# Three weight rows loaded in halves and prepared earlier, in an attention kernel with two fused MLP layers

## The chip, the cores and the metric

The kernel runs on 1 core of one Trainium2 chip. The metric is the device time of one execution in microseconds (us), as the median of repeated runs. All numbers are float32, and the matrix products are made up of float32r passes.

## What is computed

```python
# 4 batches x 8 heads x 576 positions x 64
scores = scale * q @ k.T
ret = scores * Dmat            # Dmat[n, m] = gamma_h ** (n - m) for m <= n, else 0
x = (ret @ v)                  # -> 2304 tokens x 512
h = x @ w1_in;  g = max(h, 0) + alpha * min(h, 0);  x = g @ w1_out     # 512 -> 2048 -> 512
h = x @ w2_in;  g = h * sigmoid(1.702 * h);         x = g @ w2_out     # 512 -> 2048 -> 512
```

## The kernel before

**Attention.** The 32 heads are worked in 16 pairs, numbered 0 to 15. A pair `i` has three pieces of TensorE (PE) work: `a_scores` (tile `sc`), `a_outer` (tile `st`, the running state) and `a_values` (tile `av`). The loop is staggered: in turn `i` PE does scores and outer of pair `i` and then values of pair `i-1`. VectorE (DVE) takes the scores out of PSUM (`a_evac`, tile `r`), then makes the sums of states (`a_sums`, three short instructions), then takes out the values of the pair before (`a_out`, tile `xs`). ScalarE (ACT) scales the keys (`a_keys`, tile `kts`), which the larger part of `a_outer` needs, and takes out the states. For the first eight pairs, `xa_split` also makes the two parts `x` of the result, high on ACT and the rest on DVE. The PSUM tile of `av` has one buffer, so the values of a pair can't start before `a_out` of the pair before is done. The data of pair `i+3` are asked for in turn `i` behind the values (`a_load`: `ld` of 864 KB, `kts` of 256 KB), since `ld` has four buffers.

**Weight rows.** The weights come as 64-bit floats. A row `(layer, m)` is 128 x 1024 of them (1 MB): 128 columns of the first product and 128 rows of the second. It is loaded into `raw` (two buffers) and converted with 32-bit operations, in this order: `w_abs` on ACT (called abs below), `w_clamp` on DVE (two instructions, clamps), `w_top` and `w_low` on DVE (top, low), `w_hi` on ACT (hi: the rounded high part) and `w_lo` on DVE (lo: the rest). A matmul group of 12 uses the high part in its first two matmuls and the rest in its third.

**First layer.** The steps behind the attention are numbered from 0. Step `s` does the first product of one row for one chunk of 512 tokens (`mm1`, tile `h`, 12 matmuls), the activation (two ACT instructions and one DVE instruction, tile `g`), a split of `g` into two parts (`gs`), and the second product of step `s-2` (`mm2`, tile `acc`, 12 matmuls). Steps 0 to 2 use rows 0, 1 and 2 for the first chunk. Steps 3 to 10 use rows 0 to 7 for the second, so row 3 is first used in step 6, row 6 in step 9 and row 7 in step 10. Steps 11 to 18 go back to rows 3 to 10 for the first chunk.

**Order.** Each engine works its instructions in the order in which the program gives them. The main loops stand in a fixed order. The conversions hang in a list of events with a time each (`at`), counted in pairs, then in steps from `base = 17`. `run_to(t)` works off all events up to `t`, at three places of a pair and at two of a step. All loads go through the one queue of SyncE (SP), where an instruction that waits holds up those behind it.

Of the kernel before, what the change touches and what calls it, by code (L numbers as in the profile page):

```python
# [14 lines left out]
DM, DFF = 512, 2048  # L15
# [18 lines left out]
def kernel(  # L34
# [12 lines left out]
    nc = tc.nc  # L47
# [38 lines left out]
    def at(time, fn, *args):  # L86
        events.append((time, len(events), fn, args))
# [7 lines left out]
    wt, raws, cvs, x_t = {}, {}, {}, {}  # L95
    both = "p (c n) -> p c n"

    def w_load(key, src):
        raws[key] = cvp.tile([128, 2 * DM, 2], I32, tag="raw", name="raw", bufs=2)
        nc.sync.dma_start(out=raws[key], in_=src[key[1]].rearrange("p (f t) -> p f t", t=2))  # L100

    def w_abs(key):
        cvs[key] = cvp.tile([128, 2 * DM], F32, tag="cv", name="cv", bufs=2)
# [32 lines left out]

    def w_words(t, key, src, ahead, d):
        at(t - ahead, w_load, key, src)
        for i, fn in enumerate((w_abs, w_clamp, w_top, w_low)):
            at(t + d * i, fn, key)  # L140

# [264 lines left out]
    wz = att.tile([128, 128], F32, name="wz")  # L406
    n_a = len(PAIRS)
    base = n_a + 1
    pace = [6.0, 11.0, 15.6]
    pace += [base + t for t in (1.3, 2.9, 4.5, 6.0, 7.2, 8.8, 10.6, 12.4, 14.2, 16.0, 17.8, 19.6, 22.2)]  # L410
    ahead = {0: 2.2, 1: 2.2, 2: 2.2}
    for m, t in enumerate(pace):
        d = 0.75 if m < 2 else 0.5
        w_words(t, (1, m), w1, ahead.get(m, 1.6), d)
        at(t + 3 * d + 0.25, w_hi, (1, m))
        at(t + 4 * d + 0.25, w_lo, (1, m))
# [9 lines left out]
    with tc.manual_schedule():  # L426
# [46 lines left out]
        for n, (layer, c, m0, _) in enumerate(BLOCKS[N_FIRST:], 1):  # L473
            homes[layer, c] = xp[n % 2]
            for k in range(NK):
                t = starts[layer, c, m0] - (4 if n == 1 else 6) + (0.9 if n == 1 else 1.3) * k
# [5 lines left out]
        for m in range(NM):  # L482
            t = (26.2, 29.4, 32.6)[m] if m < 3 else 35.2 + 1.6 * (m - 3) if m < 11 else 48.5 + 3 * (m - 11)
            w_words(base + t, (2, m), w2, 1.6, 0.5)
            at(base + t + 1.8, w2_store, (2, m))
            t = n1 - NM + m + LAG + 1
            at(t - 1, w2_load, (2, m))
            at(t + 0.5, w_hi, (2, m))
            at(t + 0.9, w_lo, (2, m))
# [75 lines left out]
```

## Time and profile before

| | before |
|---|---|
| median of 3 runs | 886.39 us (884.36 to 887.72) |
| the profiled execution | 891.64 us, of which the traced span is 889.6 us |
| PE busy | 871.3 us (98%) |
| DVE busy | 391.2 us (44%) |
| ACT busy | 340.5 us (38%) |
| GpSimd (POOL) busy | 174.4 us (20%) |
| bytes moved | 95.53 MB, 107 GB/s over the span |
| mean granted TensorE clock | 0.99 of full speed |

Times inside the trace are counted from the start of the span. The shares are means over the whole span. The program has stages with different limits, so a stage is read by its own rows.

### The profile page before, as it was taken

To read this page: it belongs to the slowest core of one execution; us is meant where nothing else is said; L and a number is where in the kernel's file an instruction comes from. 1 tells how busy PE (TensorE), PEld (TensorE's weight loads), DVE (VectorE), ACT (ScalarE), POOL (GpSimd) and SP (SyncE) were. 2 spreads that over 40 slices of the span, in tenths; PEclk is the share of its full clock that TensorE was granted. 3 is DMA by queue.
4 is the path that set the end of the run, shared out by engine and by line. 5 is a ranking of instruction groups with operands and counts; after the bars stand their busy time and mean duration, and the time that the engine had idled before them with its cause. 6 is when DMAs were issued, how large, how long until landed. Compare 5 with 4: busy or idle time off the path is not lost.

```text
span 889.6 us, 12276 instructions
## 1 busy us (share of the span) xinstructions
PE 871.3 (98%) x5036; PEld 739.5 (83%) x5036; DVE 391.2 (44%) x501; ACT 340.5 (38%) x602; POOL 174.4 (20%) x141
## 2 busy tenths in 40 slices
PE   8988898999999999999999999999999999999998
PEld 8877687888888888898888888888888888888898
DVE  3877686777455777572344312211221121112211
ACT  4633564554444444354455422222222222222222
POOL 0000000001222233222332322222222222222221
PEclk9989999999999999999999999999999999999999
DMA  7875652334275565642333300020002000100000
GB/s 272 319 258 199 204 186 98 143 142 142 71 249 177 161 192 191 214 167 95 107 129 106 109 1 25 0 71 1 24 0 72 1 25 0 60 1 13 23 26 24
DMA packets 30535, 95.53 MB, mean 107 GB/s; under 512 B 3600, under 2 KB 8848, under 8 KB 26000
## 3 DMA queue, kind: packets, MB, share of 16 engines
q1 hardware_dynamic: 30480, 94.76, 31.2%
q8 instruction: 39, 0.64, 0.3%
q14 instruction: 16, 0.13, 0.1%
HBM read 71.16 MB, written 23.59 MB: 107 GB/s over the span
## 4 chain that ended last, share of the span: by engine, by line
PE 89%; DVE 4%; DMA 2%; issue 2%; ACT 2%; SPq 0%; POOL 0%; ACTq 0%; DVEq 0%; POOLq 0%
PE h L326 43%; PE acc L378 42%; PE av L190 2%; DMA raw<-in_w_dram 2%; PE st L190 1%; PE sc L190 1%; DVE cv L125 1%; DMA ld<-in_qkv_dram 1%; PE wps L433 1%; DVE r L224 1%; ACT w L78 0%; DVE xs L269 0%; DVE w L81 0%; DVE cv L118 0%; POOL gs L81 0%
## 5 line engine op out<-in xcount | busy, mean ns | idle before, releaser
L326 PE MATMUL h<-x,w 128*128 128x512 f32 (+1 forms) x1920 | 423.5, 370 | 5.6 <-DVE w L81 4.1
L378 PE MATMUL acc<-gs,w 128*128 128x512 f32 (+1 forms) x1920 | 421.0, 368 | 2.1 <-ACT gs L78 1.6
L326 PEld LDWEIGHTS h<-x,w 128*128 128x128 f32 x1920 | 338.5, 190 | 67.7 <-DVE w L81 5.4
L378 PEld LDWEIGHTS acc<-gs,w 128*128 128x128 f32 x1920 | 337.0, 189 | 62.3 <-ACT gs L78 1.8
L81 POOL TENSOR_TENSOR gs<-g,gs 128x512 fp32r<-128x512 f32 (+1 forms) x137 | 174.2, 1272 | 706.9 <-ACT gs L78 591.0
L345 DVE TENSOR_TENSOR g<-h,g 128x512 f32<-128x512 f32 (+1 forms) x80 | 51.1, 638 | 299.2 <-ACT g L344 299.2
L78 ACT ACTIVATE gs<-g 128x512 fp32r<-128x512 f32 (+1 forms) x160 | 94.0, 588 | 103.0 <-DVE g L340 53.5
L344 ACT ACTIVATE g<-h 128x512 f32<-128x512 f32 (+1 forms) x80 | 44.4, 554 | 228.7 <-PE h L326 228.7
L340 DVE SCALAR_TENSOR_TENSOR g<-h,nalpha_sb,g 128x512 f32<-128x512 f32 (+1 forms) x80 | 55.6, 695 | 120.3 <-ACT h L339 120.2
L338 ACT ACTIVATE g<-h 128x512 f32<-128x512 f32 (+1 forms) x80 | 44.1, 551 | 117.7 <-PE h L326 114.6
L125 DVE SCALAR_TENSOR_TENSOR cv<-raw,cv 128x1024 int32<-128x1024 int32 x32 | 45.6, 1424 | 0.3
L104 ACT ACTIVATE cv<-raw 128x1024 f32<-128x1024 f32 x32 | 36.1, 1129 | 23.2 <-DMA raw<-in_w_dram 13.2
L81 DVE TENSOR_TENSOR x<-xf,x 128x512 fp32r<-128x512 f32 (+1 forms) x32 | 34.6, 1082 | 22.9 <-ACT x L78 22.8
L339 ACT ACTIVATE h<-h 128x512 f32<-128x512 f32 (+1 forms) x80 | 44.0, 550 | 0.0
L118 DVE SCALAR_TENSOR_TENSOR cv<-raw,cv 128x1024 int32<-128x1024 int32 x32 | 42.8, 1339 | 0.2
L108 DVE TENSOR_SCALAR cv<-cv 128x1024 f32<-128x1024 f32 x32 | 24.2, 755 | 9.6 <-ACT cv L104 9.5
L111 DVE TENSOR_SCALAR cv<-cv 128x1024 int32<-128x1024 int32 x32 | 26.4, 825 | 1.1
L78 ACT ACTIVATE w<-cv 128x1024 fp32r<-128x1024 f32 x16 | 16.9, 1057 | 22.4 <-DVE cv L125 22.4
L224 DVE TENSOR_TENSOR r<-sc,diag_sb 128x1024 f32<-128x1024 f32 x16 | 19.5, 1222 | 12.1 <-PE sc L190 11.8
L190 PE MATMUL av<-r,ld 128*64 128x128 f32 (+1 forms) x320 | 22.0, 275 | 0.0
L81 DVE TENSOR_TENSOR w<-w2f,w 128x1024 fp32r<-128x1024 f32 x16 | 19.6, 1224 | 3.6 <-ACT w L78 2.1
L190 PE MATMUL sc<-ld 64*128 64x128 f32 x256 | 19.8, 295 | 0.2 <-DMA ld<-in_qkv_dram 0.2
(38 smaller groups left out, 286.9 us busy)
## 6 DMA issues: line engine op xcount, KB each, us to landing
raw<-in_w_dram SPq DMA_DIRECT2D x32, 1024.0 KB, 6.0
ld<-in_qkv_dram SPq DMA_DIRECT2D x15, 864.0 KB, 6.3
w<-cv SPq DMA_DIRECT2D x16, 512.0 KB, 6.7
w2f<-w SPq DMA_DIRECT2D x16, 512.0 KB, 3.4
kts<-in_kn_dram SPq DMA_DIRECT2D x16, 256.0 KB, 5.8
xf<-x SPq DMA_DIRECT2D x16, 256.0 KB, 3.4
out_dram<-o SPq DMA_DIRECT2D x16, 256.0 KB, 4.2
part<-pt SPq DMA_DIRECT2D x3, 1024.0 KB, 5.0
```

What stands on the lines that cost most here:

```text
L78: return nc.scalar.activation(out=out, in_=in_, func=ACTF.Copy)
L81: return eng.tensor_tensor(out=out, in0=a, in1=b.bitcast(F32), op=ALU.subtract)
L118: nc.vector.scalar_tensor_tensor(out=g, in0=raws[key][:, :, 1], scalar=-(1 << 30), in1=g, op0=ALU.bitwise_and, op1=ALU.bitwise_or,)
L125: nc.vector.scalar_tensor_tensor(out=g, in0=raws.pop(key)[:, :, 0], scalar=29, in1=g, op0=ALU.logical_shift_right, op1=ALU.bitwise_or,)
L190: nc.tensor.matmul(out=out, lhsT=lhsT, rhs=rhs, start=start, stop=stop, skip_group_check=True)
L326: nc.tensor.matmul(out=t, lhsT=w[:, cw, k * 128:k * 128 + 128], rhs=x[:, cx], start=(i == 0), stop=(i == 3 * NK - 1),)
L338: nc.scalar.activation(out=g, in_=t, func=ACTF.Relu)
L339: nc.scalar.activation(out=t, in_=t, func=ACTF.Relu, scale=-1.0)
L340: nc.vector.scalar_tensor_tensor(out=g, in0=t, scalar=nalpha_sb[:, m:m + 1], in1=g, op0=ALU.mult, op1=ALU.add)
L344: nc.scalar.activation(out=g, in_=t, func=ACTF.Sigmoid, scale=1.702)
L345: nc.vector.tensor_tensor(out=g, in0=t, in1=g, op=ALU.mult)
L378: nc.tensor.matmul(out=acc[0][d], lhsT=w[:, cw, d * 128:d * 128 + 128], rhs=g[:, cx], start=(j == m0 and i == 0), stop=(j == m1 - 1 and i ...
```

## The change

Each row of weights is loaded by two transfers of 512 KB instead of one of 1 MB. For rows 0, 1 and 2 the second transfer is asked for one pair after the first. For all others both stand directly behind one another. The list of times for the first layer's rows is another: rows 0, 1 and 2 move from 6.0, 11.0 and 15.6 pairs to 3.6, 8.6 and 14.1, rows 3 to 7 move by 0.2 to 0.6 steps, and rows 12 to 15 by 0.1 to 0.8. Row 2 gets the wider spacing of its operations that rows 0 and 1 have.

```diff
     def w_load(key, src):
         raws[key] = cvp.tile([128, 2 * DM, 2], I32, tag="raw", name="raw", bufs=2)
-        nc.sync.dma_start(out=raws[key], in_=src[key[1]].rearrange("p (f t) -> p f t", t=2))
+        w_piece(key, src, 0)
+
+    def w_piece(key, src, c):
+        f = src[key[1]].rearrange("p (f t) -> p f t", t=2)
+        nc.sync.dma_start(out=raws[key][:, c * DM:c * DM + DM], in_=f[:, c * DM:c * DM + DM])
...
     def w_words(t, key, src, ahead, d):
         at(t - ahead, w_load, key, src)
+        at(t - ahead + (1.0 if ahead > 2 else 0), w_piece, key, src, 1)
...
-    pace = [6.0, 11.0, 15.6]
-    pace += [base + t for t in (1.3, 2.9, 4.5, 6.0, 7.2, 8.8, 10.6, 12.4, 14.2, 16.0, 17.8, 19.6, 22.2)]
-    ahead = {0: 2.2, 1: 2.2, 2: 2.2}
+    pace = [3.6, 8.6, 14.1]
+    pace += [base + t for t in (0.8, 2.35, 3.9, 5.45, 7.0, 8.8, 10.6, 12.4, 14.2, 15.9, 17.6, 19.3, 21.4)]
+    ahead = {0: 2.6, 1: 3.2, 2: 3.2}
     for m, t in enumerate(pace):
-        d = 0.75 if m < 2 else 0.5
+        d = 0.75 if m < 3 else 0.5
```

PE's order of matmuls is the same in both. Three places show how the others move. The first is SP's queue at the start of the attention, before: `ld_187` belongs to pair 3, and the row of weights stands behind the loads of pair 6.

```order
L167 DMA ld_187<-in_qkv_dram 128x1728
L168 DMA kts_116<-in_kn_dram 128x512
L167 DMA ld_245<-in_qkv_dram 128x1728
L168 DMA kts_116<-in_kn_dram 128x512
L167 DMA ld_305<-in_qkv_dram 128x1728
L168 DMA kts_116<-in_kn_dram 128x512
L167 DMA ld_368<-in_qkv_dram 128x1728
L168 DMA kts_116<-in_kn_dram 128x512
L100 DMA raw_387<-in_w1_dram 128x2048
```

The same queue in the change, again from pair 3's load on.

```order
L172 DMA ld_187<-in_qkv_dram 128x1728
L173 DMA kts_116<-in_kn_dram 128x512
L104 DMA raw_206<-in_w1_dram 128x1024
L172 DMA ld_247<-in_qkv_dram 128x1728
L173 DMA kts_116<-in_kn_dram 128x512
L104 DMA raw_206<-in_w1_dram 128x1024
L172 DMA ld_308<-in_qkv_dram 128x1728
L173 DMA kts_116<-in_kn_dram 128x512
```

The first half of row 0 now stands behind pair 3's loads and the second behind pair 4's.

The second place is DVE around row 0, in the change. It begins with the values of pair 3 (`xs_432`), the clamps of row 0 (`cv_377`) and the scores of pair 5 (`r_453`), and ends with low.

```order
L274 TENSOR_TENSOR xs_432<-av_413,otab_sb_82 128x576
L112 TENSOR_SCALAR cv_377<-cv_377 128x1024
L115 TENSOR_SCALAR cv_377<-cv_377 128x1024
L81 TENSOR_TENSOR x_439<-xs_245,x_439 128x64
L229 TENSOR_TENSOR r_453<-sc_442,diag_sb_80 128x1024
L81 TENSOR_TENSOR x_455<-xs_432,x_455 128x512
...
L122 SCALAR_TENSOR_TENSOR cv_377<-raw_206,cv_377 128x1024
L274 TENSOR_TENSOR xs_432<-av_474,otab_sb_82 128x576
L81 TENSOR_TENSOR x_499<-xs_432,x_499 128x64
L229 TENSOR_TENSOR r_513<-sc_502,diag_sb_80 128x1024
L129 SCALAR_TENSOR_TENSOR cv_377<-raw_206,cv_377 128x1024
```

Before, the clamps of row 0 stood ahead of the scores of pair 7, and low stood two pairs further on. On ACT the copy hi of row 0 (`w_531`) now stands ahead of the keys of pair 7, here in the change:

```order
L181 ACTIVATE r_513<-st_516,vtab_sb_78 128x320
L78 ACTIVATE w_531<-cv_377 128x1024
L78 ACTIVATE x_311<-xs_432 128x448
L181 ACTIVATE kts_116<-kts_116,vtab_sb_78 128x4x64 x2
L181 ACTIVATE r_570<-st_573,vtab_sb_78 128x320
```

Before, it stood at the same place of a turn two pairs later, ahead of the keys of pair 9.

The third place is DVE at the end of the attention, before: the values of pairs 14 and 15 (`xs_925`, `xs_1051`), row 2 (`cv_1028`) and the first activation (`g_1078`).

```order
L269 TENSOR_TENSOR xs_925<-av_1008,otab_sb_82 128x576
L108 TENSOR_SCALAR cv_1028<-cv_1028 128x1024
L111 TENSOR_SCALAR cv_1028<-cv_1028 128x1024
L269 TENSOR_TENSOR xs_1051<-av_1032,otab_sb_82 128x576
L118 SCALAR_TENSOR_TENSOR cv_1028<-raw_927,cv_1028 128x1024
L462 TENSOR_SCALAR nalpha_sb_84<-alpha_sb_83 128x16
L340 SCALAR_TENSOR_TENSOR g_1078<-h_1065,nalpha_sb_84,g_1078 128x512
L125 SCALAR_TENSOR_TENSOR cv_1028<-raw_927,cv_1028 128x1024
L81 TENSOR_TENSOR gs_1085<-g_1078,gs_1085 128x512
L81 TENSOR_TENSOR w_1083<-cv_1028,w_1083 128x1024
```

The same place in the change; row 2 is `cv_963` and its rest `w_1061`.

```order
L229 TENSOR_TENSOR r_996<-sc_985,diag_sb_80 128x1024
L112 TENSOR_SCALAR cv_963<-cv_963 128x1024
L115 TENSOR_SCALAR cv_963<-cv_963 128x1024
...
L274 TENSOR_TENSOR xs_933<-av_1015,otab_sb_82 128x576
L122 SCALAR_TENSOR_TENSOR cv_963<-raw_791,cv_963 128x1024
L274 TENSOR_TENSOR xs_1058<-av_1039,otab_sb_82 128x576
L129 SCALAR_TENSOR_TENSOR cv_963<-raw_791,cv_963 128x1024
L467 TENSOR_SCALAR nalpha_sb_84<-alpha_sb_83 128x16
L345 SCALAR_TENSOR_TENSOR g_1085<-h_1072,nalpha_sb_84,g_1085 128x512
L81 TENSOR_TENSOR w_1061<-cv_963,w_1061 128x1024
```

Row 2's clamps moved to between the scores and the sums of pair 15, top ahead of the last values, low ahead of the first activation, and lo ahead of its split.

## Rows read from the trace of the kernel before

**Rows 1.** Windows: first and third of three stretches; busy PE, PEld, DVE, ACT, POOL, granted clock, DMA share, GB/s.

```profile
13.97:85.48 71.51, 66.49 (x1118) 57.92 (x1117) 57.31 (x99) 34.30 (x78) 0.00 (x0) 0.95 0.74 270
...
148.07:889.60 741.53, 736.38 (x3601) 625.22 (x3599) 285.36 (x341) 269.31 (x466) 174.20 (x137) 1.00 0.25 84
```

**Rows 2.** Chain in order of time: start, us, what; undisturbed pair and matmul groups.

```profile
20.03 2.06 PE av L190 x36
22.09 1.09 PE sc L190 x16
23.18 0.88 PE st L190 x20
...
85.48 2.96 PE h L326 x12
...
101.69 2.72 PE h L326 x12
```

**Rows 3.** Waits of PE: total us, times, longest.

```profile
PE h L326 <- DVE w L81: 4.1, 3, 1.6
PE st L190 <- ACT kts L176: 3.8, 2, 2.6
```

**Rows 4.** Chain at the end of row 0, from low on.

```profile
47.63 1.15 DVE cv L125
...
48.80 1.06 ACT w L78
49.85 0.47 ACT x L78
...
50.77 1.51 PE st L190 x16
52.29 3.81 PE av L190 x36
56.09 1.56 PE sc L190 x16
```

**Rows 5.** Windows of 4 us behind two waits of PE; columns as in rows 1.

```profile
52.00:56.00 4.00, 4.00 (x40) 3.46 (x37) 2.15 (x5) 1.79 (x4) 0.00 (x0) 0.50 0.46 186
72.00:76.00 4.00, 2.71 (x48) 2.14 (x43) 3.46 (x6) 1.85 (x3) 0.00 (x0) 1.00 1.03 364
```

**Rows 6.** Chain: DVE's instructions in a row, each up to the next one's start.

```profile
39.47 0.53 DVE x L81
...
65.42 0.61 DVE cv L108
...
66.06 0.69 DVE cv L111
66.75 1.13 DVE r L224
...
68.73 0.71 DVE xs L269
```

**Rows 7.** Window ahead of the first weights; columns as in rows 1.

```profile
16.00:20.00 4.00, 4.00 (x75) 3.51 (x74) 2.86 (x6) 3.50 (x10) 0.00 (x0) 1.00 0.32 98
```

**Rows 8.** Loads issued in 18:19 us: KB each, us to landing.

```profile
ld<-in_qkv_dram SPq DMA_DIRECT2D x1, 864.0 KB, 4.3
kts<-in_kn_dram SPq DMA_DIRECT2D x1, 256.0 KB, 4.5
```

**Rows 9.** Chain: row 0's load, from issue to landing.

```profile
27.01 9.22 DMA raw<-in_w_dram
```

**Rows 10.** Timeline of SP: the issue of that load.

```profile
27.01 0.42 SPq L100 DMA_DIRECT2D raw<-in_w_dram  x1
```

**Rows 11.** Chain: step 0's `g`, and step 2's remaining ten matmuls.

```profile
89.63 0.75 DVE g L340
...
95.03 3.93 PE h L326 x10
```

**Rows 12.** Timeline of ACT: the keys of pair 4.

```profile
25.48 0.89 ACT L176 ACTIVATE kts<-kts,vtab_sb 128x256 f32<-128x256 f32 x2
```

## The prediction

> **What bounds the kernel now.** I read the windows of three stretches first [rows 1]: the attention from 13.97 to 85.48 us, the first steps up to 148.07, and the rest. In the third PE is busy for 736.4 of 741.5 us at the full clock: it is bound by PE, and as PE's matmuls stay the same there is nothing to win there. The other two stretches hold the losses.
>
> *Attention, 13.97 to 85.48.* In the chain an undisturbed pair is scores 1.09, outer 0.88, values 2.06, so 4.03 us [rows 2]. Fifteen pairs and the last values make 15 x 4.03 + 2.06 = 62.5, which would end at 76.5. The end is at 85.48: 9.0 us are lost.
>
> *First steps, 85.48 to 148.07.* In them lie 11 first and 9 second products of 12 matmuls. One takes 2.72 (the first of all 2.96) [rows 2]: 54.6 of 62.6. So 8.0 us are lost.
>
> Next I read what PE waited for [rows 3]: 3.8 us in two waits of outer for the keys from ACT, and 4.1 us in three waits of the first product for lo. The chain shows how the longest wait of the attention comes about [rows 4]. ACT's hi stands ahead of the keys in ACT's queue and needs low from DVE. Low ended at 48.78, hi took 1.06, the split 0.47, then came the keys, and outer could go on at 50.77. PE stood idle before that for 2.6, the longest of the two waits [rows 3]. Behind this wait the granted clock was 0.50 (1.2 GHz) from 52 to 56 [rows 5]: values took 3.81 instead of 2.06, scores 1.56 instead of 1.09, the outer's last 16 matmuls 1.51 instead of 0.7 (16/20 of 0.88), in sum 3.0 us. The second of these waits (3.8 - 2.6 = 1.2) lies in 72 to 76, where the clock stayed at 1.00.
>
> **The change, part by part.**
>
> *Loads.* The same bytes in two transfers. Between 16 and 20 us the DMA engines are busy for only 0.32 [rows 7], and the first half of row 0 now waits there. The second stands behind pair 4's loads, which go out when pair 0's values are done, at 13.97 + 4.03 = 18.0; issues stand 0.42 apart [rows 10], so 18.0, 18.4 and 18.9. The 864 KB of that pair land at 18.0 + 4.3 = 22.3, the 256 KB behind them at 18.4 + 4.5 = 22.9 [rows 8]: 0.6 for 256 KB, so a half row lands about 1.3 later, at 24.2. ACT reaches abs at 25.48, where it took up pair 4's keys before [rows 12]. The next pair's loads go out a pair later, at 22.0, so they find the queue nearly free. A pair asks for 1120 KB, which by that rate take 2.7 of its 4.03 us; a half row of 1.3 just fits in the gap. Before, the whole MB took 9.22 [rows 9] and stood ahead of three pairs' loads. I put the loads at 0. Upper bound: each of the six halves delays a pair by its full 1.3, 7.8 us; lower bound 0. I take 0, as the rows nearest to it are those of a queue that runs empty.
>
> Here a rule speaks against the change. The Trainium skill, "DMA: Bandwidth & Descriptors", section "Rules for kernel authors", asks for 1 MB or more per transfer, and the section on the anatomy of a DMA gives about 2.0 us as fixed cost of each. If 32 more transfers paid it on the path, that would be an estimated 64 us. The trace does not agree for a transfer that follows another: the 0.6 us above hold no such cost.
>
> *Row 0 (pairs 4 to 7).* DVE's pieces, from [rows 6]: clamps 66.75 - 65.42 = 1.33, `r` 1.13, the sums 68.73 - 66.75 - 1.13 = 0.85, `xs` 0.7; low 1.15 [rows 4], and top and lo on the same 1024 columns also 1.15; on ACT hi 1.06 and the split 0.47 [rows 4], the keys 0.89 [rows 12]; a split of 448 columns is 0.53, so 0.6 for 512 and 0.1 for 64. Two points matter for PE: values of pair i are asked for 1.09 + 0.88 = 1.97 after the scores of i+1 start, and need `xs` of the pair before; the keys are asked for about 1.3 after the scores start (1.09 and some 0.2 for four of the outer's 20 matmuls, an estimate from its 0.88).
> Abs, on 1024 columns like hi, puts pair 4's keys at 25.48 + 1.06 + 0.89 = 27.4, where they are asked for (pair 4's scores start at 26.06 = 13.97 + 3 x 4.03): some **0.1**. Pair 5's scores start at 30.2, pair 6's at 34.2. DVE: `xs` of pair 3 ends at 31.1, clamps 32.4, split 32.5, `r` 33.6, split 34.2, sums 35.1, top 36.2, `xs` 36.9. Values of pair 5 were asked for at 36.2: **0.7 waited**. Pair 7 starts at 39.0. DVE goes on: split 37.0, `r` 38.2, low 39.3. On ACT hi ends at 40.4, the split at 40.8, the keys at 41.7; asked for at 40.3: **1.4 waited**. Then DVE catches up. Pair 8 starts at 44.4 (keys 41.7, 0.7 for the outer's rest, values 2.06), pair 9 at 48.4, pair 10 at 52.5.
>
> *Row 1 (pairs 9 to 12).* The same order without the splits from pair 8 on. `xs` of pair 8 ends at 53.3, clamps 54.6, split 55.1, `r` 56.2, sums 57.1, top 58.2, `xs` 58.9, asked for at 56.5 + 1.97 = 58.5: **0.4**. Pair 12 starts at 61.0. Then `r` 60.0, low 61.2, hi 62.2, keys 63.1, asked for at 62.3: **0.8**.
>
> *Row 2 (pair 15).* Its clamps now stand between `r` and sums. Pair 13 starts at 65.8, and pair 15 at 73.9: `r` ends at 76.2, clamps 77.5, sums 78.4, `xs` of pair 14 79.0. The last values are asked for at 77.9: **1.1**.
>
> Sum of waits 0.1 + 0.7 + 1.4 + 0.4 + 0.8 + 1.1 = 4.5, each below the 2.6 that brought the clock down. The attention ends at 76.5 + 4.5 = 81.0 instead of 85.48: **4.4 gained**. Bounds: no wait left, 9.0; as late as before, 0. I take the sum along the queues, since the order on each engine is known and the durations hardly vary.
>
> *First steps.* Call the end of the attention A. Before, low of row 2 stood behind the first `g`, so hi and lo came late, step 2 got its lo at 95.0, and ten matmuls took 3.93 instead of 2.27 at the lowered clock [rows 11]. Now low ends at A + 0.8 + 1.15 = A + 1.9, hi at A + 3.0, the first `g` at A + 4.9 (1.94 behind its product, as before: 90.38 - 88.44, [rows 2, 11]) and lo at A + 6.05. Step 2 starts at A + 2.96 + 2.72 = A + 5.7 and needs lo for its third matmul, 2 x 0.227 later, at A + 6.1: no wait, just. The other two waits for lo, 2.5 together (4.1 - 1.6, [rows 3]), are rows 6 and 7 in steps 9 and 10. Step k starts at A + 11.1 + 5.44 (k - 3). In DVE's new order row 6 has behind `g` of step 7 (A + 37.5) clamps of row 7, the split of `g` (0.6 for 512 columns) and its lo: A + 40.6, wanted at A + 44.2. Row 7's lo stands behind `g` of step 9, which ends 1.94 behind its product, at A + 48.4: A + 49.6, wanted at A + 49.7, just in time. So the 8.0 come back: **8.0 gained**; bounds 5.5 (those 2.5 stay) and 8.0.
>
> *The rest.* SP issues 29 halves more at 0.42 each; PE, busy throughout the third stretch [rows 1], covers SP's time there. I take 0; without that cover it is at most the 12.2 us of 29 x 0.42.
>
> **Sum.** 4.4 + 8.0 = 12.4. The span becomes 889.6 - 12.4 = 877.2, the profiled execution (2.0 more than its span) 891.6 - 12.4 = 879.2. That execution lay 5.25 above the median of the runs, so for the median 886.4 - 12.4 = 874.0.
>
> **Rivals.**
> 1. *The clock falls in pair 7.* The waits of 0.7 and 1.4 lie 4 us apart and might work like one of 2.6. Price 3.0 [rows 4], so 877.0. For it: the waits come close together; against: a single 1.2 cost nothing [rows 5]. The Trainium skill, "TensorE: Matmul & The Clock Gate", Part 1, says that idleness halves the clock and activity restores it; both rows fit that.
> 2. *The change doesn't do what it says in the attention.* A late half row makes abs wait, ACT is late with the keys as before, and the 9.0 stay: only the 8.0 come back, 878.4. For it: a load took 9.22 here [rows 9]; against: half the bytes behind a short queue.
> 3. *All waits vanish.* DVE has more air than I count: 9.0 + 8.0, so 869.4.
> 4. *The halves hold up the pairs' loads*, 7.8 of the 12.4 given back: 881.8. Against it: the idle share [rows 7].
> 5. *Slower: the doubled transfers of the later rows reach the path.* SP is one queue, and weights, stores and chunk loads stand in it. With 29 more transfers at the 0.42 of an issue each the gain is gone (12.2 of 12.4); from 0.57 each on it is over 0.5% slower, and at 1.0 each 886.4 - 12.4 + 29 = 903. For it: all loads share SP; against: DMA share of 0.25 there [rows 1].
>
> **How the numbers follow.** Forecast 0.52, rivals 0.15, 0.10, 0.12, 0.07 and 0.04. 0.5% is 4.4 us, about what a measurement of this kernel can tell from no change. The forecast and rivals 1 to 3 lie beyond it, 0.89, of which I take off 0.02 for mixtures; rival 4 lies on the edge. So faster 0.87, same 0.08, slower 0.05. The range reaches from rival 3 at 869.5 over rival 2 to 880, leaving out rivals 4 and 5 and half of rival 3.
>
> **What would show it.** Right: abs of row 0 starts at about 25.5 without waiting for its load; PE waits once for `xs` and once for keys in pairs 6 and 7, none over 1.5; granted clock 1.00 from 36 to 80; attention ends near 81; step 2 does not wait for lo, nor do steps 9 and 10; step 11 starts 12 us sooner. Wrong: a wait over 2 us with a granted clock of 0.50 behind it, loads of pairs 5 to 12 that take over 8 us, or new waits of PE behind step 11.

## The result, and the profile after

The changed kernel takes 877.31 us (median of 4 runs, 875.46 to 879.47); the kernel before, beside it on the same chip, 886.19 (884.36 to 887.72). The ratio is 0.9901 with a 95% interval of 0.9872 to 0.9931: 8.9 us faster, between 6.1 and 11.3. The forecast of 874.0 is 3.3 too low; the time lies in the range, on the side that was forecast.

The profiled execution took 877.74 us, with a span of 876.0. The windows of the changed kernel, cut at the same places as [rows 1] (the attention; the first steps up to step 11; the rest), with the same columns:

```profile
13.41:81.92 68.51, 64.31 (x1117) 55.63 (x1117) 58.10 (x100) 34.22 (x78) 0.00 (x0) 1.00 0.80 282
81.92:137.16 55.24, 55.24 (x241) 45.09 (x242) 45.12 (x56) 31.71 (x47) 0.00 (x0) 1.00 0.53 181
137.16:876.00 738.84, 734.73 (x3600) 623.56 (x3599) 285.00 (x341) 268.99 (x465) 173.99 (x137) 1.00 0.25 85
```

And the kernel before, cut behind the attention at exactly these places:

```profile
85.48:148.23 62.75, 57.16 (x241) 45.97 (x242) 46.39 (x57) 31.75 (x47) 0.00 (x0) 0.97 0.46 156
148.23:889.60 741.37, 736.22 (x3600) 625.06 (x3599) 285.20 (x341) 269.23 (x465) 174.20 (x137) 1.00 0.25 84
```

The span is 13.6 us shorter: 0.6 by an earlier start of the scores (13.41 in the chain's times, where the kernel before has 14.04; [rows 1] cut it 0.07 earlier), 2.9 in the attention, 7.5 in the first steps, 2.5 in the rest, where nothing was forecast. PE counts as busy for every moment of the first steps now, and the granted clock is 1.00 (2.4 GHz) in all three.

What PE waited for in the changed kernel (us in total, times, longest), beside [rows 3]:

```profile
PE st L195 <- ACT kts L181: 2.2, 4, 0.9
PE av L195 <- DVE xs L274: 2.1, 3, 1.3
...
PE acc L383 <- ACT gs L78: 0.5, 1, 0.5
PE acc L383 <- POOL gs L81: 0.5, 1, 0.5
```

In this view the first product `h` waits for nothing any more, and the wait for keys of 2.6 is gone; several of 0.2 to 1.3 have taken its place (0.4 of the 2.2 lies in the start-up). Where they lie, the timeline of PE shows (start, length; in brackets the idle time and its releaser). The first row is the scores of pair 5, and an undisturbed pair has its scores 4.03 behind the last:

```profile
29.52 1.16 PE L195 MATMUL sc<-ld 64*128 64x128 f32 x16
...
33.55 1.16 PE L195 MATMUL sc<-ld 64*128 64x128 f32 x16
...
35.07 1.08 PE L195 MATMUL st<-ld,kts 128*64 128x64 f32 x16
36.37 0.99 PE L195 MATMUL av<-ld,r 64*64 64x128 f32 x16 [0.22 <-DVE xs L274]
...
38.43 1.16 PE L195 MATMUL sc<-ld 64*128 64x128 f32 x16
...
40.72 1.08 PE L195 MATMUL st<-ld,kts 128*64 128x64 f32 x16 [0.87 <-ACT kts L181]
...
43.79 1.16 PE L195 MATMUL sc<-ld 64*128 64x128 f32 x16
...
47.81 1.16 PE L195 MATMUL sc<-ld 64*128 64x128 f32 x16
...
49.86 1.07 PE L195 MATMUL st<-ld,kts 128*64 128x64 f32 x16 [0.62 <-ACT kts L181]
...
52.92 1.16 PE L195 MATMUL sc<-ld 64*128 64x128 f32 x16
...
59.50 0.99 PE L195 MATMUL av<-ld,r 64*64 64x128 f32 x16 [0.51 <-DVE xs L274]
...
63.25 1.08 PE L195 MATMUL st<-ld,kts 128*64 128x64 f32 x16 [0.27 <-ACT kts L181]
...
79.79 0.99 PE L195 MATMUL av<-ld,r 64*64 64x128 f32 x16 [1.33 <-DVE xs L274]
```

From one row of scores to the next are 4.88, 5.36, 4.02 and 5.11: a wait for keys costs PE more than the idle time in the bracket, as the 16 outer matmuls behind it take 1.08 instead of 0.69. In pair 6 two waits cover each other: its keys were late too, as ScalarE's timeline shows, and ended the outer product 0.56 late, but the values behind it had to wait for `xs` until 36.37 in any case.

```profile
34.51 0.91 ACT L181 ACTIVATE kts<-kts,vtab_sb 128x256 f32<-128x256 f32 x2 [2.23 <-DMA kts<-in_kn_dram]
```

The wait at 49.86 has its cause in the chain:

```profile
39.40 8.77 DMA raw<-in_w_dram
...
48.25 1.16 ACT cv L108
49.41 0.80 ACT kts L181 x2
```

The second half of row 1 left at 39.40 and landed 8.8 us later; abs stood still for it, and pair 9's keys stood behind abs in ScalarE's queue.

### The profile page after: what moved, and what is told of

It is laid out like the page before. It is cut to its first block, busy times and chain, and to the rows that moved or that the text cites. A ratio compares the mean times of both kernels' runs of the same rounds, so it can differ in the third digit from the quotient of the medians.

```text
span 876.0 us, 12331 instructions
## 1 busy us (share of the span) xinstructions
PE 865.2 (99%) x5036; PEld 734.4 (84%) x5036; DVE 390.5 (45%) x501; ACT 340.2 (39%) x602; POOL 174.2 (20%) x141
## 4 chain that ended last, share of the span: by engine, by line
PE 91%; issue 3%; DVE 2%; DMA 1%; POOL 1%; ACT 1%; SPq 0%; POOLq 0%; ACTq 0%; DVEq 0%
PE h L331 43%; PE acc L383 43%; PE av L195 2%; POOL gs L81 1%; DMA raw<-in_w_dram 1%; PE st L195 1%; PE sc L195 1%; DVE r L229 1%; PE wps L438 0%; DVE xs L274 0%; DMA vtab_sb<-in_vtab_dram 0%; DVE cv L122 0%; DVE cv L115 0%; ACT kts L181 0%; DVE cv L112 0%
## 5 line engine op out<-in xcount | busy, mean ns | idle before, releaser
L108 ACT ACTIVATE cv<-raw 128x1024 f32<-128x1024 f32 x32 | 36.2, 1131 | 30.4 <-DMA w<-cv 11.3
```

## The experiments

All times are medians, with ratios to the kernel before on the same chip. "The end of the attention" is the start of the first `h` in the profile's timeline of PE.

**Split alone.** The changed kernel with the old times: only the loads differ from before.

```diff
-    pace = [3.6, 8.6, 14.1]
-    pace += [base + t for t in (0.8, 2.35, 3.9, 5.45, 7.0, 8.8, ...)]
-    ahead = {0: 2.6, 1: 3.2, 2: 3.2}
+    pace = [6.0, 11.0, 15.6]
+    pace += [base + t for t in (1.3, 2.9, 4.5, 6.0, 7.2, 8.8, ...)]
+    ahead = {0: 2.2, 1: 2.2, 2: 2.2}
...
-        d = 0.75 if m < 3 else 0.5
+        d = 0.75 if m < 2 else 0.5
```

> The kernel before with its own times, but every row loaded in two halves (for rows 0 to 2 a pair apart). My theory (the times at which rows are converted matter, the halves don't): 886, within 1.5 us of the kernel before, and the attention still loses about 9 us with a wait over 2 us for the keys. Rival theory (the halves keep the pairs' loads from being held up): 877 to 880, and the keys of the pair behind row 0 are no longer late.

891.08 us, ratio 1.0056 (1.0038 to 1.0073): slower, which neither expected. On ScalarE's timeline abs of row 0 stands still for its load:

```profile
37.49 1.12 ACT L108 ACTIVATE cv<-raw 128x1024 f32<-128x1024 f32 x1 [6.01 <-DMA raw<-in_w_dram]
```

And PE's waits, with a new one for `r`:

```profile
PE st L195 <- ACT kts L181: 4.8, 3, 2.2
...
PE st L195 <- ACT r L181: 1.9, 1, 1.9
```

The half that goes out a pair later holds up abs; behind abs stands `r`, for which the outer product of the next pair now waits 1.9. The halves alone don't help, and at the old times cost 4.2 us.

**Whole loads at the new times.** The changed kernel with one transfer of 1 MB per row.

```diff
-        w_piece(key, src, 0)
+        nc.sync.dma_start(out=raws[key], in_=src[key[1]].rearrange("p (f t) -> p f t", t=2))
...
-        at(t - ahead + (1.0 if ahead > 2 else 0), w_piece, key, src, 1)
```

> The changed kernel with its times, but every row in one transfer of 1 MB. My theory: 877 to 879, at most 1.5 us slower than the changed kernel, from a load of pair 4 or 5 that lands late. Rival theory: most of the gain is gone, 883 or more, with loads of pairs 5 to 12 over 8 us.

877.64, ratio 0.9894 (0.9874 to 0.9914). As the theory said: the times do it, the halves give nothing measurable. In the profile they even cost something: the attention lasts 67.4 with whole loads (13.57 to 80.99) against 68.5, because row 1's load is in time and pair 10's scores stand 4.03 behind pair 9's instead of 5.11. The last short block of the first layer, of which more below, waits longer there, 1.5 instead of 0.5.

**Rows 0 to 2 moved alone.** The changed kernel with the old times of the later rows.

```diff
-    pace += [base + t for t in (0.8, 2.35, 3.9, 5.45, 7.0, 8.8, ...)]
+    pace += [base + t for t in (1.3, 2.9, 4.5, 6.0, 7.2, 8.8, ...)]
```

> The changed kernel, with the times of rows 3 to 15 put back. My theory: the waits of steps 9 and 10 for lo come back, 2.4 us, so 879.5 to 880; attention and step 2 as in the changed kernel. Rival theory (the times of the later rows carry the gain): 884 or more.

879.78, ratio 0.9923 (0.9906 to 0.994), in the expected interval. Its waits hold the two of the first product for lo, in steps 9 and 10, again:

```profile
PE h L331 <- DVE w L81: 2.4, 2, 1.3
```

**Later rows moved alone.** The other half: old times for rows 0 to 2, in halves.

```diff
-    pace = [3.6, 8.6, 14.1]
+    pace = [6.0, 11.0, 15.6]
...
-    ahead = {0: 2.6, 1: 3.2, 2: 3.2}
+    ahead = {0: 2.2, 1: 2.2, 2: 2.2}
...
-        d = 0.75 if m < 3 else 0.5
+        d = 0.75 if m < 2 else 0.5
```

> The changed kernel, with the times of rows 0 to 2 put back, in halves all the same. My theory: the attention loses about 9 us again and step 2 waits for row 2 again, so only some 2.4 us are gained: 883.5 to 884. Rival theory: 878 to 880.

888.06, ratio 1.0008 (0.9991 to 1.0025): missed by 4 us, because the expectation took the halves as free. Against the split alone, its proper neighbour, the later rows gave 3.0; against the pair of runs above 2.5 (879.78 - 877.31), or 2.0 by their ratios. So of the gain some 2 to 3 belongs to the later rows, the bulk to rows 0 to 2.

**hi behind the keys.** ScalarE's queue holds pair k's hi ahead of the next keys; now behind.

```diff
-        at(t + 3 * d + 0.25, w_hi, (1, m))
+        at(t + 3 * d + (0.95 if m < 2 else 0.25), w_hi, (1, m))
```

> The changed kernel, but the hi copies of rows 0 and 1 stand behind the next pair's key scalings on ScalarE instead of ahead of them; nothing else moves. Theory (the state products' waits of 0.87 and 0.27 us for the keys at 40.7 and 63.3 us are time on the path, and ScalarE stands idle for over 2 us ahead of either hi, so the keys take nothing from it): both waits vanish, the end of the attention comes 0.9 to 1.1 us earlier (about 80.9), and the median is 1.0 us under the changed kernel's 877.3, about 876.3. Rival (VectorE's chain of low word, sums and lo is what holds the pair up, and the wait only moves one step on, to the last values): the attention still ends at 81.7 to 81.9 and the median is 877.0 to 877.5.

876.03, ratio 0.987 (0.9843 to 0.9897). The attention lasts 66.9 us (12.11 to 78.97) instead of 68.5, and ScalarE's timeline shows the keys done before the hi begins, so that the keys of pairs 7 and 12 are no longer late: the scores behind these two stand 4.02 and 4.03 apart instead of 5.36 and 4.76. (Waits of 0.2 for the keys of pair 4 and 0.3 for those of pair 9 remain.) The median alone, 1.3 lower, would not show it, as the two intervals overlap.

```profile
36.17 0.89 ACT L181 ACTIVATE kts<-kts,vtab_sb 128x256 f32<-128x256 f32 x2
38.08 1.06 ACT L78 ACTIVATE w<-cv 128x1024 fp32r<-128x1024 f32 x1 [1.02 <-DVE cv L129]
```

**Halves of rows 0 to 2 together, and row 1's halves a pair earlier.** Two kernels that remove the wait for row 1's second half in two ways:

```diff
-        at(t - ahead + (1.0 if ahead > 2 else 0), w_piece, key, src, 1)
+        at(t - ahead, w_piece, key, src, 1)
```

> The changed kernel, but the two halves of rows 0 to 2 go out together at the first half's place; the halves of all later rows stay as they are. Theory (the pair between the halves is what makes row 1's words late, 1.32 us on ScalarE, and what the halves gave came in the first layer's last short block, where a row of the second layer landed in 6.6 us instead of 8.9): the abs of row 1 waits under 0.3 us, the attention ends at about 81.1 as with whole loads, the wait of the accumulation in the last short block stays at 1.0 us or below, and the median is 876.3 to 876.8. Rival (the halves a pair apart are what spares the pairs' own loads, and both halves together hold up the next loads as the whole loads did at the old times): the scores or keys wait over 1 us more, attention end 83 or later, median 878 to 879.

```diff
-    ahead = {0: 2.6, 1: 3.2, 2: 3.2}
+    ahead = {0: 2.6, 1: 4.2, 2: 3.2}
```

> The changed kernel, but both halves of row 1 go out one pair earlier; the pair between them stays. Theory (the second half's landing at 48.2 us is what row 1's abs, and behind it the keys and state products, wait for): the 1.32 us of ScalarE and the 0.62 us of the state products at 49.9 vanish, the attention ends at about 81.2, median 876.6. Rival (the transfer is late because the pairs' loads stand in the same rings; moved forward it delays a pair's keys by as much): the wait of the state products for the keys stays at 2 us in sum, median 877.0 to 878.

878.48 (ratio 0.9897, 0.9872 to 0.9922) and 875.89 (0.9872, 0.9847 to 0.9898). In both abs of row 1 starts without a wait, here in the first:

```profile
48.95 1.15 ACT L108 ACTIVATE cv<-raw 128x1024 f32<-128x1024 f32 x1
```

In the second the scores of pairs 8 to 11 stand 4.03 apart, so the 1.08 between pairs 9 and 10 is gone, as the theory has it. Within the attention the waits for keys sum to 1.1 in the first and 1.5 in the second, against the changed kernel's 1.8, so the rivals' mechanism, more waiting or as much, isn't there, though in the first the rival's time is. The medians can't decide. In the profiled executions, 2.7 apart, the start makes the difference: the scores start at 15.47 in the first and at 12.01 in the second, while the attention lasts 67.4 and 68.1, the other way round. The second's is the longer because an early start is paid for in part: abs of row 0 then comes before the second half of its load and waits 0.57 for it, and pair 4 loses 0.8. (In the kernel with hi behind the keys, which started at 12.11, the same wait is 0.46.)

**Both, and row 7 half a step earlier.**

```diff
-        at(t - ahead + (1.0 if ahead > 2 else 0), w_piece, key, src, 1)
+        at(t - ahead, w_piece, key, src, 1)
...
-    pace += [base + t for t in (0.8, 2.35, 3.9, 5.45, 7.0, 8.8, ...)]
+    pace += [base + t for t in (0.8, 2.35, 3.9, 5.45, 6.5, 8.8, ...)]
...
-        at(t + 3 * d + 0.25, w_hi, (1, m))
+        at(t + 3 * d + (0.95 if m < 2 else 0.25), w_hi, (1, m))
```

> Both edits, hi behind the keys and the halves of rows 0 to 2 together, and row 7 of the first steps half a step earlier (its lo was 0.3 us late at 131.4). Theory (the three gains are on the path and add up, 1.1, 0.8 and 0.3): attention end about 80.1, no stall of h at 131, median 875.1 to 875.5. Rival (one waiting engine hides the next, so that the gains don't add): 876.2 to 877.0. A time of 877.3 or more would say that the new order costs something that none of the single edits shows.

875.44, ratio 0.9863 (0.9836 to 0.9889). The attention lasts 65.5, and the product at step 10 no longer takes 3.02 but 2.72: the gains add up there. Some of it went at a place that the expectation had left out, the last short block of the first layer. On PE's timeline, the kernel before:

```profile
369.53 0.50 PE L378 MATMUL acc<-gs,w 128*128 128x256 f32 x2 [1.60 <-ACT gs L78]
370.54 2.09 PE L378 MATMUL acc<-gs,w 128*128 128x256 f32 x10 [0.50 <-POOL gs L81]
372.43 2.51 PE L326 MATMUL h<-x,w 128*128 128x256 f32 x12
```

The changed kernel there:

```profile
357.38 0.50 PE L383 MATMUL acc<-gs,w 128*128 128x256 f32 x2 [0.51 <-ACT gs L78]
358.38 1.46 PE L383 MATMUL acc<-gs,w 128*128 128x256 f32 x10 [0.50 <-POOL gs L81]
```

And this version:

```profile
355.65 0.50 PE L383 MATMUL acc<-gs,w 128*128 128x256 f32 x2 [1.24 <-ACT gs L78]
356.65 2.32 PE L383 MATMUL acc<-gs,w 128*128 128x256 f32 x10 [0.50 <-POOL gs L81]
358.77 2.28 PE L331 MATMUL h<-x,w 128*128 128x256 f32 x12
```

PE waits for ScalarE's copy of `gs`, which stands behind an abs of the second layer's row 12, which waits for its load. In the kernel before:

```profile
368.06 1.12 ACT L104 ACTIVATE cv<-raw 128x1024 f32<-128x1024 f32 x1 [5.12 <-DMA raw<-in_w_dram]
369.07 0.41 ACT L78 ACTIVATE gs<-g 128x256 fp32r<-128x256 f32 x1
```

Where the wait is long, matmuls behind it run slower (2.09 and 2.32 for the ten that take 1.46 in the changed kernel, 2.51 and 2.28 for twelve that take 1.60). My theory had put its shrinking from 1.60 to 0.51 down to the halves. That fell: this kernel and the one with hi behind the keys load in halves and wait 1.24 and 1.16.

**Row 12 ahead of the stores.** Its load stands in SP's queue behind four x stores that wait for the accumulation, here in the kernel before:

```profile
357.09 2.03 SPq L403 DMA_DIRECT2D x<-o  x4
359.17 1.18 SPq L100 DMA_DIRECT2D raw<-in_w_dram  x1
```

It goes ahead of them, once in the kernel before and once in the joint version:

```diff
-            w_words(base + t, (2, m), w2, 1.6, 0.5)
+            w_words(base + t, (2, m), w2, 2.8 if m == 12 else 1.6, 0.5)
```

> The kernel before with one edit: the load of the second layer's row 12 goes out ahead of the four x stores of the first layer instead of behind them (its step 48.7 instead of 49.9 after the attention); the attention and the first steps stay. Theory (that load, landing 8.9 us after its issue at 359 us, is what the last short block's accumulation waited for, 1.60 us and 0.50 us, and the clock fell behind it): the wait of the accumulation for ScalarE's gs vanishes, and the median is 1.5 to 2.5 us under the kernel before's, about 884.7. Rival (the transfers of that stretch are slow wherever the load is put, or the wait is for VectorE): the wait stays at 1.2 us or above and the median is that of before, 886 to 887.

> The earlier joint version (hi behind the keys, halves of rows 0 to 2 together, row 7 half a step earlier) with the same edit, the second layer's row 12 ahead of the x stores. Theory (the same wait of 1.2 us in that version's profile): no wait of the accumulation for gs in the last short block, median 873.4 to 874.2 against the joint version's 875.4. Rival (that wait comes and goes with the executions and costs little on average): 875.0 to 875.6.

885.45, ratio 0.9984 (0.9963 to 1.0006), and 872.49, ratio 0.9836 (0.9813 to 0.986). In the profile of the first the load goes out at 350.95, ahead of the stores at 355.40. In both the wait for `gs`, POOL's part with it, is gone, and the rest from step 11 on is the same to 0.2 us, 4.1 and 1.7 below the kernels before and after. The kernel before with this edit, the rest:

```profile
146.54:883.80 737.26, 734.21 (x3600) 623.50 (x3599) 285.22 (x341) 269.59 (x465) 174.17 (x137) 1.00 0.25 85
```

The joint version with it:

```profile
135.28:872.40 737.12, 734.03 (x3600) 623.43 (x3598) 285.25 (x341) 269.37 (x465) 173.98 (x137) 1.00 0.26 85
```

In the kernel before the median moved by 1.9, and its interval still holds no change; in the joint version by 2.9 from one measurement to the next, 2.4 by the ratios. The mechanism is shown by the profiles, the size over many executions only as about 2 to 3.

**Words behind the values.** The joint version with row 12, and rows 0 and 1 with a whole pair between their steps, so that VectorE's words stand behind `xs`.

```diff
-        d = 0.75 if m < 3 else 0.5
+        d = (1.0, 1.0, 0.75)[m] if m < 3 else 0.5
...
-        at(t + 3 * d + (0.95 if m < 2 else 0.25), w_hi, (1, m))
+        at(t + 3 * d + 0.25, w_hi, (1, m))
```

> As the one before, and the steps of rows 0 and 1 a whole pair apart (d 1.0 instead of 0.75), so that VectorE's clamps, top and low words each stand behind the last operation on a pair's values instead of ahead of it. Theory (the waits of the values product for VectorE's output of the pair before, 0.79 us at 37 us and 0.51 us at 58 us, are the top words of rows 0 and 1 that stand ahead of it): both vanish, attention 1.1 to 1.3 us shorter, median 872.2 to 873.0. Rival (VectorE has no room in these pairs, the clamps and words then hold up the next scores' eviction or the sums): waits of 0.5 us or more turn up at other pairs and the median stays within 0.5 us of the version without it.

871.29 (870.35 to 871.82), ratio 0.9817 (0.9794 to 0.9841), the best here, some 6 us under the changed kernel and 0.9 under the expected interval. The attention missed its 1.1 to 1.3 a little (65.54 to 64.61): both waits are gone, but pair 8, whose keys now come 0.2 late, loses 0.6 instead of 0.2. All that PE waits for behind the start-up is:

```profile
PE av L195 <- DVE xs L274: 1.3, 1, 1.3
...
PE st L195 <- ACT kts L181: 0.2, 1, 0.2
```

**The kernel before, profiled again.** Unchanged.

> The kernel before, unchanged, profiled a second time. Theory (the first profiled execution of it, 891.64 us, was 5.25 us over the median because it lost more than the others to the lower clock and to the wait of the last short block, so that losses read from it can't be taken off the median whole): a profiled execution of 885 to 888 us, in which the values of pair 7 or the ten matmuls behind step 2's lo take less than the 3.81 and 3.93 us of the first, or the accumulation of the last short block waits less than 1.60 us for gs. Rival (those losses are in every execution, and the first one was long only in its start-up): the same rows within 0.2 us, and the difference lies ahead of the first scores at 13.97 us.

Median 889.9 beside 888.55, ratio 1.0 (0.997 to 1.0031); the profiled execution took 890.20, not the 885 to 888 of the theory. In its rows the theory is half right. The keys of pair 9, behind row 0's hi, come 2.70 late on PE's timeline, the values behind them, pair 8's (the expectation calls them pair 7's), take 2.96 (52.87 to 55.83) instead of 3.81, and step 2's ten matmuls 2.60 instead of 3.93; but the last short block waited longer:

```profile
51.42 1.52 PE L190 MATMUL st<-ld,kts 128*64 128x64 f32 x16 [2.70 <-ACT kts L176]
...
94.39 2.60 PE L326 MATMUL h<-x,w 128*128 128x512 f32 x10 [1.65 <-DVE w L81]
...
368.33 0.50 PE L378 MATMUL acc<-gs,w 128*128 128x256 f32 x2 [2.37 <-ACT gs L78]
```

By windows:

```profile
15.16:84.82 69.66, 64.72 (x1117) 56.51 (x1117) 57.30 (x99) 34.29 (x78) 0.00 (x0) 0.98 0.75 269
84.82:146.25 61.43, 55.87 (x242) 44.93 (x242) 46.39 (x57) 31.81 (x47) 0.00 (x0) 1.00 0.47 160
```

The same instructions lose 1.8 less in the attention and 1.3 less in the first steps than in the first profile, and the rest is 0.6 longer.

## Why the prediction was right, and where it missed

The forecast of the span, 877.2 for a measured 876.0, is closer than its parts, and that is luck: 2.0 of the 12.4 did not come (1.5 in the attention, 0.5 in the first steps), and 3.1 came where nothing was forecast (0.6 by the start, 2.5 in the rest).

*Waits of the attention.* The five waits of the sum that needed a place on PE are there, at the pairs named. By the distances of the scores: 0.85 for 0.7 (values of pair 5), 1.33 for 1.4 (keys of pair 7), 0.57 for 0.4 and 0.73 for 0.8 (row 1), 1.4 for 1.1 (the last values), and nearly nothing (0.08) for the 0.1 at pair 4: 5.0 for 4.5. So the order on ScalarE and VectorE with durations of before was enough to place them. That hi ahead of the keys and row 1's late half cost time is shown by the kernels that took them away; top ahead of `xs`, by the last version.

*Loads at 0.* Mis-sized: 1.08, the late half of row 1. The first half of row 0 took 9.0 and the second 5.9, the latter in time for abs, which started at 24.85 unhindered. The 1.3 for half a row held: row 1's second half landed 1.2 behind the keys that stand ahead of it. What did not hold is the short queue, the 4.3 and 4.5 of [rows 8] for a pair's own loads. Ahead of that half they took:

```profile
ld<-in_qkv_dram SPq DMA_DIRECT2D x1, 864.0 KB, 7.8
kts<-in_kn_dram SPq DMA_DIRECT2D x1, 256.0 KB, 8.0
```

The trace of the kernel before has this already: the loads of pairs 5 to 9 took 6.3 to 8.4 there, and [rows 8] show pair 4's alone. The keys of pair 6 took 8.5 in the changed kernel, one of the signs of being wrong, and cost nothing only because the values behind them waited longer for `xs`. The other reading of rival 4, that halves are dear, is true at the old times (4.2 us) and not at the new ones. The Trainium skill, "DMA: Bandwidth & Descriptors", section "Rules for kernel authors", asks for 1 MB or more per transfer; whole loads at the new times took 877.64 against 877.31, so for time on the path the rule made no difference here.

*Clock (rival 1) and the other rivals.* Waits up to 1.33 left the granted clock at 1.00 throughout the attention. The price of 3.0 was 0.4 too high: the outer's 16 matmuls take 1.08 behind a late key at the full clock too, so of their 1.51 only 0.4 was the clock's. Rival 3 fell with the waits that stayed, and rival 2 with the 3.0 that the attention gave. Rival 5, the doubled transfers on the path, is answered by whole loads at the new times, which were no faster. What fell away with the wait of 2.6 is its slow stretch.

*First steps.* 7.5 for 8.0. Row 2's "no wait, just" and row 7's "just in time" each missed by a little, and each cost 0.3: steps 0 to 2 take 8.70 instead of 2.96 + 2 x 2.72 = 8.40, and step 10 takes 3.02. VectorE's lo of row 2 ended at 88.00, and step 2's third matmul, due at 87.9, started at 88.06.

```profile
81.92 8.70 PE h L331 x36
...
131.42 3.02 PE h L331 x12
```

*The rest at 0.* Wrong in the profiled execution: 2.5. "PE busy for 736.4 of 741.5, nothing to win there" overlooked that a busy PE includes matmuls at the lower clock (736.22 before, 734.03 in the joint version with row 12 earlier), and that 5 us idle is not nothing. The change did not aim at it: in the eleven profiles without the edit to row 12 this wait was 0 to 2.4, and over 1 us both with halves and without. That it is a race between row 12's load and the x stores is shown by the edit that ends it; why it came out at 0.51 in the changed kernel's execution stays open.

*From the span to the median.* This is the step that missed by most: "for the median 886.4 - 12.4 = 874.0". The two profiled executions lie 13.9 apart (891.64 and 877.74), the medians 8.9. The losses were those of one execution that lay 5.25 above the median, and were taken whole from the median. The second profile of before loses 7.2 (69.66 - 62.5) in the attention instead of 9.0, and its first steps are 1.3 shorter. With these the same sums give 2.7 + 6.7 = 9.4, and 877.0. So much of the miss is the size of the clock's losses, which vary. The other executions agree: beside the kernels with row 12 earlier, the kernel before took 882.47 and 883.70 with a mean granted clock of 1.00 and 889.57 and 889.72 with one of 0.990, the clock of the execution whose losses were taken. How much of the 3.3 it makes stays open: the second profile stood 0.3 above the median of its own runs, 889.9, and those runs were slower than the forecast's 886.4.

## What to carry to other kernels

- Lay out the queue of each in-order engine for the slot where a new piece of work stands, and put it behind the operation that PE waits for, not ahead: the same hi, moved behind the keys, and the same top, moved behind `xs`, each took waits off PE (2.1 and 1.4 us in the attention) and put back less (0.2 and 0.4, at pair 8).
- A load queued behind stores that wait for results is late by that wait, so put it ahead of them. That is also the Trainium skill's "DMA: Bandwidth & Descriptors", "Rules for kernel authors", to issue early and wait late, and row 12 agrees: the wait, 1.6 and 2.4 in the two profiles of the kernel before and 1.2 in the joint version, is gone in both kernels that have the edit.
- Profile the kernel before twice before a loss is subtracted from a median: step 2's ten matmuls behind the same wait took 3.93 in one execution and 2.60 in the other.

## What was not expected of the hardware

Behind equal waits the clock falls in one execution and not in another: step 2's ten matmuls, behind the same waits of 1.51 and 1.65, took 3.93 and 2.60 in two executions of before, 4.14 in the split alone, 2.56 with row 12 earlier. In the two long ones the mean granted clock of 5 us around them is 0.66, in the two short ones 1.00. In the short block, waits for `gs` of 1.16 to 2.37, each with POOL's 0.50 behind it, were followed by slower matmuls in every profile that has them (2.76 for twelve that take 1.60, in the kernel with hi behind the keys, at a granted clock of 0.50), 1.04 and less by none; and 1.33 ahead of the last values was not followed by any.

The six halves of rows 0 to 2, 512 KB each, took 5.9 to 9.0 us in one execution. The scores of pair 1, ruled by the first loads, started between 11.83 and 15.47 us in the 14 profiles, a spread of 3.6 us that no edit here was meant to make; two profiles of the unchanged kernel alone, 13.97 and 15.09, lie 1.1 apart.
